# Key sums of six batches turned by a transposing DMA instead of TensorE, in a fused linear-attention and MoE kernel

## Chip, cores and metric

One Trainium2 chip, one core. The metric is the device time of one launch in microseconds (us). Most executions of a kernel agree within 0.3%. Engines are called PE (TensorE), DVE (VectorE), ACT (ScalarE), Pool (GpSimd) and SP (the queue that issues most DMAs).

## The reference

```python
def phi(x):                       # 8 batches, 8 heads, 576 tokens, 64 wide, 128 features
    proj = einsum('bhsd,md->bhsm', x, omega)
    h = proj - sum(x * x, -1, keepdims=True) / 2
    h = h - max(h, -1, keepdims=True)
    return exp(h) / sqrt(m)
q_p, k_p = phi(q * scale), phi(k * scale)
kv = einsum('bhsm,bhsd->bhmd', k_p, v)      # the key sums
z = sum(k_p, axis=2)
attn = einsum('bhsm,bhmd->bhsd', q_p, kv) / (einsum('bhsm,bhm->bhs', q_p, z)[..., None] + 1e-6)
x = attn as (4608 tokens, 512)
logits = xn @ en.T / tau          # rows of x and expert_emb (8 experts) normalized
idx = argmax(logits); gate = softmax(logits)[idx]
out[t] = gate[t] * relu(x[t] @ w1[idx[t]]) @ w2[idx[t]]       # 512 -> 1024 -> 512
```

## The kernel before

**Two stages.** In the first, the attention runs over 36 tiles of 128 tokens, four superblocks of nine tiles, each of two batches; its rows of x are scattered to memory by expert. In the second, the experts run over 38 steps of 128 sorted rows. The change touches the first stage alone.

**One pass of the loop.** Pass i works on the keys of tile i and on the queries of tile i - 7. From pass 7 to pass 35 PE projects both query halves (line 374), turns the query features of the tile before (`qtr`, line 462), projects both key halves, adds one half of the heads of tile i - 1 to the key sums (`kvmm`, line 406), multiplies turned query features with finished key sums (`num`, line 482) and adds the other half of the heads. DVE takes the row maxima (line 378) and divides (`num_out`, lines 495 to 501); ACT does the exponentials (line 388, sixteen a pass) and a copy (line 467). Pool does the routing in small pieces (`routed`) and scatters one tile's rows a pass (line 570). SP issues the loads of keys, values and queries some two passes ahead, as buffers come free.

**The key sums.** A batch (a "half", b = 0 or 1, of superblock sb) is complete behind pass i = 5, 9, 14, 18, 23, 27, 32 and 36. `kv_out` (line 420) then copies its sums from PSUM into the tile `kvs`: 128 features by 8 heads by 64 sums, the denominator, and 8 columns that hold the product of the sums with the normalized expert rows, so that `num` gives numerators, denominator and expert logits together. For these 8 columns the sums have to be turned, from features by channels to channels by features, two heads at a time: `kv_dense` (Pool, line 424) packs 64 of each 73 columns into the tile `xgp[2]`; two passes later, `kv_turn` (PE, line 433, four transposes into a PSUM bank), `kv_turned` (DVE, line 437, one copy back to `xgp[2]`), `kv_logits` (PE, line 444, sixteen small products) and `kv_logits_out` (DVE, line 450, into `kvs`). Pass i + 2 is called the turning pass here: passes 11, 16, 20, 25, 29 and 34 for the six halves of the change. They begin at 39.93, 67.11, 88.12, 115.16, 136.16 and 165.53 us.

**Order.** PE, Pool and SP run their instructions as written; DVE and ACT too inside the loop. Work that isn't done at once is put into lists, `early`, `spare`, `mid` and `ends`, keyed by pass and slot, and `go` runs a list: `early` at the start of a pass, `ends` at its end. In a turning pass PE has `kv_turn` between the first `kvmm` and `num`, and `kv_logits` right behind `num`. The scatter of a pass (line 570) is written in `ends`, so it stands on Pool's queue ahead of whatever `early` of the next pass brings. `xgp[0]` is free from pass 7 to pass 35.

Of the kernel before, what the change touches and what calls it, by code (L numbers as in the profile page):

```python
# [15 lines left out]
U16 = mybir.dt.uint16  # L16
# [6 lines left out]
P = 128  # L23
B, H, S, D, M = 8, 8, 576, 64, 128
E, F = 8, 1024
N = B * S
DM = H * D
# [12 lines left out]
NPRE = 2  # L40
# [24 lines left out]
def attention_moe(ctx: ExitStack, tc: tile.TileContext, qT, kT, v1, omT, emb, tau, w1q, w2q, xs, out):  # L65
    nc = tc.nc
# [56 lines left out]
    first = const.tile([P, 1], F32, name="first")  # L123
    firsti = const.tile([P, NPRE + 2], I32, name="firsti")
    xgp = [const.tile([P, PAY], F32, name=f"xgp{t}") for t in range(NPRE + 1)]
# [197 lines left out]
    with ExitStack() as c1:  # L323
# [5 lines left out]
        kva, kvs, st = {}, {}, {}  # L329
# [5 lines left out]
        def load(i):  # L335

            if i >= NTILE:
                return
            if i == LAG - 1:
                st["k", i] = xgp[0][:, 0:DM].rearrange("p (c m) -> p c m", c=4)  # L340
            else:
                st["k", i] = p1.tile([P, 4, P], F32, name=f"kt{i}", tag="qt" if i in (2, 3) else "kt", bufs=2)
            nc.sync.dma_start(st["k", i], kT[i])
# [17 lines left out]
        def loadq(i):  # L361
            if 0 <= i < NTILE:
                st["q", i] = p1.tile([P, 4, P], F32, name=f"qt{i}", tag="kt" if i in QLOADS[NTILE][1:] + QLOADS[NTILE + 1] else "qt", bufs=2)
                nc.sync.dma_start(st["q", i], qT[i])
# [3 lines left out]
        def proj(*which):  # L368
            for w, i, a, k in which:
                st["pj" + w, i, a] = (pb[k] if isinstance(k, int) else k).rearrange("p (c m) -> p c m", c=4)  # L370
            for c in range(4):
                for w, i, a, _ in which:
                    r = slice(a * D, (a + 1) * D)
                    nc.tensor.matmul(st["pj" + w, i, a][:, c, :], st[w, i][r, c, :], om[r, :], start=True, stop=True)  # L374
# [39 lines left out]
        def kv_out(sb, b):  # L414
            for a in range(2):
                to, acc = kvs[sb, b][:, 4 * a : 4 * a + 4, 0 : D + 1], kva[sb, b, a]
                if (sb, b) == (0, 0):
                    nc.vector.tensor_copy(to, acc)
                else:
                    nc.scalar.activation(to, acc, AF.Copy)  # L420
# [14 lines left out]
        def kv_turned(sb, b):  # L435
            kvt = xgp[NPRE][:, 0:DM].rearrange("p (c m) -> p c m", c=4)
            nc.vector.tensor_copy(kvt.rearrange("p c m -> p (c m)"), st["kvb"])
            st["kvt", sb, b] = kvt

        def kv_logits(sb, b):  # L440
            st["kve", sb, b] = pe = nu[1][:, 424 : 424 + 8 * E].rearrange("p (c e) -> p c e", c=4)
            for c in range(4):
                for o in range(0, P, 64):
                    nc.tensor.matmul(
                        pe[o : o + 64, c], st["kvt", sb, b][:, c, o : o + 64], enbd[:, c].rearrange("p a e -> p (a e)"),
                        start=True, stop=True,
                    )
# [148 lines left out]
        def first_weights(n):  # L596

            if n == 0:
                st["fe"] = nc.values_load(firsti[0:1, NPRE + 1 :], engines=[ET.SP], min_val=0, max_val=E - 1, skip_runtime_bounds_check_because=WHY)
            q, wn = n // 2, ("w1", "w2")[n % 2]  # L600
            st["rf", n] = raw = rawp.tile([P, F], F32, name=f"rf{n}", tag=f"raw_{wn}")
            nc.sync.dma_start(raw, W[wn][0].rearrange("(e q) p f -> e q p f", q=NQ)[ds(st["fe"], 1), q].rearrange("o p f -> (o p) f"))
# [123 lines left out]
        early, spare, mid, ends, behind = {}, {}, {}, {}, []  # L726
# [9 lines left out]
        def go(d, *key):  # L736
            for f, *a in d.pop(key, ()):
                f(*a)
# [6 lines left out]
        loop.enter_context(tc.manual_schedule(engines={ET.DVE, ET.Activation}))  # L745
        for i in range(NTILE + LAG + 2):
            iq = i - LAG
            for n in QLOADS.get(i, () if i >= NTILE else (iq + 2,) if i >= LAG else (i - 4,)):
                loadq(n)
            ahead = i + (4 if i < 2 else 2)  # L750
            if i < 2 or i > 4:
                load(ahead)
            if i in LOADS:
                first_weights(LOADS[i])
            if i == 1 or i >= 4:
# [10 lines left out]
            ks, qs = i < NTILE, 0 <= iq < NTILE  # L766
            st["both"] = ks
            sb, u = divmod(i - 1, TPS)
# [10 lines left out]
            if ks and qs:  # L779
                if i > LAG:  # L780
                    proj(q1 + (3,), q0 + (1,))
                if turns:
                    qtr(iq - 1, *nu)
                maxima(*q1)
                if turns:
                    qcopy(iq - 1, 1)
                    qcopy(iq - 1, 0, True)
                maxima(*q0)
                go(spare, i, 4)
                feats(*q1)  # L790
                feats(*q0)
                proj(k1 + (2,), k0 + (0,))
                maxima(*k1)
                maxima(*k0)
                kv(1)
                if u == 4:
                    kv(0)
                    kv_out(sb, 0)
                go(spare, i, 3)
                slot(4)  # L800
                if sums:
                    num(iq - 1)
                go(spare, i, 0)
                go(spare, i, 1)
                slot(2)
                if u == 4:
                    kv(0, 1, b=1)
                else:
                    kv(0)
                if sums:  # L810
                    num_out(iq - 1)
                feats(*k1)
                feats(*k0)
                slot(0)
                slot(1)
            elif ks:
                for j in KPROJ.get(i, ()):
                    proj(*keys(j))
                if i == LAG - 1:
                    proj(("q", 0, 1, 3), ("q", 0, 0, 1))  # L820
                go(spare, i, 0)
                maxima(*k0)
                maxima(*k1)
                slot(0)
                if i == LAG - 1:
                    kv_out(0, 0)
                    kv_dense(0, 0)
                    for a in range(2):
                        kvmm(i - 2, a, 1)
                    kv(0, 1)  # L830
                    kv_turn(0, 0)
                    emb2()
                else:
                    kv(0, 1)
                slot(1)
                feats(*k0)
                go(spare, i, 1)
                feats(*k1)
                slot(2)
            else:  # L840
                mine, other = ((3, 1), (0, 2))[:: 1 if i % 2 == NTILE % 2 else -1]
                if qs:
                    proj(q1 + (mine[0],), q0 + (mine[1],))
                kv(1)
                go(spare, i, 2)
                slot(3)
                if turns:
                    qtr(iq - 1, *(pb[k] for k in other))
                kv(0)
                if sums:  # L850
                    num(done)
                go(spare, i, 0)
                if i == NTILE + 1:
                    flush()
                if qs:
                    maxima(*q1)
                    maxima(*q0)
                if i > NTILE and turns:
                    qcopy(iq - 1, 0, True)
                if qs:  # L860
                    feats(*q1)
                if i == NTILE:
                    kv_out(sb, 1)
                    qcopy(iq - 1, 0, True)
                if qs:
                    feats(*q0)
                if turns:
                    qcopy(iq - 1, 1)
                if sums:
                    num_out(done)  # L870
                flush()
                filled(1)
                slot(0)
                slot(1)
                filled(FILLS[i] - 1)
                go(spare, i, 1)
                slot(2)
            if sums and done % G == G - 1:
# [16 lines left out]
                for n, (d, *key) in enumerate(plan):  # L895
                    todo = at(d, *key) if key[0] < NTILE + LAG + 2 else behind
                    todo.insert(0 if n == 0 else len(todo), (next, steps, None))
            go(ends, i)
            if 0 <= i - 1 < NTILE and u in (4, 8):
                b = u // 4 - 1  # L900
                if b and ks:
                    kv_out(sb, b)
                k = int(not ks)
                if i + 2 == LAG:
                    todo = (kv_turned, spare, i + 2, 4), (kv_logits, spare, i + 2, 3), (kv_logits_out, mid, i + 2, 4)
                else:
                    kv_dense(sb, b)
                    todo = (kv_turn, spare, i + 2, 3 - k), (kv_turned, mid, i + 2, 4 - k)
                    todo += (kv_logits, spare, i + 2 + k, 0), (kv_logits_out, mid, i + 2 + k, 0)
                for f, *key in todo:  # L910
                    at(*key).append((f, sb, b))
# [184 lines left out]
    with tc.manual_schedule(engines={ET.PE, ET.Activation, ET.DVE, ET.Pool, ET.SP}):  # L1096
# [82 lines left out]
        for t in range(NPRE, NSTAT):  # L1179
# [10 lines left out]
            early = late and (t < SHIFT or t == ends)  # L1190
# [105 lines left out]
    with tc.If(tot > NSTAT):  # L1296
        with tc.For_i(NSTAT, tot, 1) as i:
            get = lambda k, eng, mx: nc.values_load(tabi[k : k + 1, ds(i, 1)], engines=[eng], min_val=0, max_val=mx, skip_runtime_bounds_check_because=WHY)
            xgl = x_of("x", get(0, ET.SP, DUM))
            src = get(2, ET.SP, E * NQ - 1)  # L1300
# [65 lines left out]
```

## Time and profile before

| | |
|---|---|
| median of 3 runs | 640.89 us (640.69 to 641.74) |
| profiled execution | 637.09 us, span from first to last instruction 635.4 us |
| PE, DVE, ACT, Pool busy | 98%, 77%, 68%, 66% of the span |
| first stage | to about 200 us |

The profile shows one execution. Its busy shares are means over both stages, so a term of the first stage has to be read from the stretches there.

### The profile page before, as it was taken

How to read it: one execution, taken by the hardware profiler on the slowest of the kernel's cores; microseconds unless marked ns; L12 is line 12 of the kernel's file. 1: busy time of each engine (PE TensorE's matmuls, PEld its weight loads, DVE VectorE, ACT ScalarE, POOL GpSimd, SP SyncE). 2: the span in 40 equal slices, each digit the busy share in tenths (PEclk: the TensorE clock that was granted, in tenths of full speed). 3: DMA queues.
4: the chain of work that ended last, by engine and by line, in shares of the span. 5: the costliest groups of instructions: out<-in, count | busy, mean ns of one | idle time of the engine just before them, and what ended most of it. 6: DMA issues, size and time to landing. Idle time of an engine off the chain costs nothing.

```text
span 635.4 us, 19064 instructions
## 1 busy us (share of the span) xinstructions
PE 622.5 (98%) x6293; PEld 532.9 (84%) x6294; DVE 490.5 (77%) x908; ACT 433.2 (68%) x1139; POOL 421.9 (66%) x603
## 2 busy tenths in 40 slices
PE   8999999999999899999999999999999999999996
PEld 8999999988878788888888888888888888888885
DVE  5788888888879834797778776888877787878754
ACT  6999899898998327665666675666575657576630
POOL 3013344455777734579787888989797979787962
PEclk9999999999999999999999999999999999999999
DMA  7654766767682377798978687787878686868631
GB/s 257 210 149 158 231 202 200 222 200 256 233 289 80 142 267 233 233 230 224 214 222 230 206 227 223 204 244 191 243 191 239 198 243 188 239 203 223 198 117 46
DMA packets 142239, 131.93 MB, mean 208 GB/s; under 512 B 106742, under 2 KB 106870, under 8 KB 142144
## 3 DMA queue, kind: packets, MB, share of 16 engines
q1 hardware_dynamic: 135520, 109.70, 60.1%
q0 software_dynamic: 6480, 20.91, 8.6%
q8 instruction: 57, 0.93, 0.6%
q14 instruction: 38, 0.31, 0.1%
q10 hardware_dynamic: 144, 0.07, 0.0%
HBM read 83.78 MB, written 21.97 MB: 166 GB/s over the span
## 4 chain that ended last, share of the span: by engine, by line
PE 69%; ACT 3%; DVE 2%; issue 0%; POOL 0%; ACTq 0%; DVEq 0%
PE pb L285 31%; PE po L285 31%; PE fs_o L285 2%; PE pb L374 1%; ACT ftq L388 1%; PE nuu L482 1%; PE pb L267 1%; PE fs_a L285 1%; PE kva L406 1%; DVE nmq L378 0%; PE pb L462 0%; ACT qp L467 0%; DVE xr L501 0%; DVE rt_p L299 0%; DVE qp L469 0%
## 5 line engine op out<-in xcount | busy, mean ns | idle before, releaser
L240 POOL TENSOR_TENSOR w2l<-raww,w2h 128x256 f32 x128 | 144.4, 1128 | 7.6
L240 POOL TENSOR_TENSOR w1l<-raww,w1h 128x256 f32 (+1 forms) x130 | 112.9, 869 | 14.0 <-DMA xgp<-xs 4.8
L285 PE MATMUL po<-w2h,hh 128*128 (+1 forms) x288 | 112.2, 390 | 0.0
L285 PE MATMUL po<-w2h,hl 128*128 (+1 forms) x288 | 112.1, 389 | 0.0
L285 PE MATMUL po<-w2l,hh 128*128 (+1 forms) x288 | 112.0, 389 | 0.0
L285 PE MATMUL pb<-w1h,xh 128*128 (+1 forms) x280 | 109.4, 391 | 0.0
L285 PE MATMUL pb<-w1h,xl 128*128 (+1 forms) x280 | 109.0, 389 | 0.0
L285 PE MATMUL pb<-w1l,xh 128*128 (+1 forms) x280 | 109.0, 389 | 0.0
L1086 DVE COPY pl<-pb 128x512 uint16<-128x512 uint16 x68 | 46.8, 690 | 61.5 <-ACT pl L1082 61.4
L1082 ACT ACTIVATE pl<-pb 128x512 uint16<-128x512 uint16 x68 | 39.5, 586 | 75.4 <-PE pb L285 71.3
L388 ACT ACTIVATE ftq<-pb,nmq 128x128 f32<-128x128 f32 x288 | 79.7, 414 | 2.2 <-DVE nmq L378 2.2
L315 POOL DMA_INDIRECT y<-xgp,tail x36 | 44.9, 1247 | 53.3 <-DVE w1h L234 29.5
L388 ACT ACTIVATE ftk<-pb,nmk 128x128 f32<-128x128 f32 x272 | 75.9, 460 | 4.8 <-DVE nmk L378 4.8
L1104 DVE COPY wd<-t 128x1024 uint16<-128x1024 uint16 x68 | 65.0, 959 | 1.3 <-DMA t<-pl 1.2
L1120 ACT ACTIVATE hh<-wd 128x1024 fp32r<-128x1024 f32 x34 | 36.1, 1063 | 42.4 <-DVE wd L1104 37.4
L285 PEld LDWEIGHTS po<-w2h,hl 128*128 128x128 f32 x288 | 54.1, 188 | 11.3
L285 PEld LDWEIGHTS po<-w2h,hh 128*128 128x128 f32 x288 | 54.1, 188 | 11.2
L285 PEld LDWEIGHTS po<-w2l,hh 128*128 128x128 f32 x288 | 54.0, 188 | 11.0
L285 PEld LDWEIGHTS pb<-w1h,xl 128*128 128x128 f32 x280 | 52.5, 188 | 10.9
L285 PEld LDWEIGHTS pb<-w1h,xh 128*128 128x128 f32 x280 | 52.6, 188 | 10.9
L285 PEld LDWEIGHTS pb<-w1l,xh 128*128 128x128 f32 x280 | 52.6, 188 | 10.7
L1124 DVE SCALAR_TENSOR_TENSOR hl<-wd,hh 128x1024 fp32r<-128x1024 f32 x34 | 54.2, 1594 | 4.0 <-ACT hh L1120 3.4
(341 smaller groups left out, 1242.9 us busy)
## 6 DMA issues: line engine op xcount, KB each, us to landing
raww<-w1q SPq DMA_DIRECT2D x38, 512.0 KB, 4.0
raww<-w2q SPq DMA_DIRECT2D x38, 512.0 KB, 4.8
qt<-qT SPq DMA_DIRECT2D x36, 256.0 KB, 4.1
kt<-kT SPq DMA_DIRECT2D x35, 256.0 KB, 3.6
xg<-xs SPq DMA_DIRECT2D x23, 260.5 KB, 2.8
xgp<-xs SPq DMA_DIRECT2D x15, 260.5 KB, 4.8
rf<-w1q SPq DMA_DIRECT2D x4, 512.0 KB
rf<-w2q SPq DMA_DIRECT2D x4, 512.0 KB
```

Of the source, the lines that this page charges most:

```text
L240: ils.append(eng.tensor_tensor(at(l, d)[:, c], raw[:, c], at(h, d)[:, c].bitcast(F32), op=ALU.subtract))
L267: nc.tensor.transpose(bank[:, c * P : (c + 1) * P], src[:, o + c * P : o + (c + 1) * P], ident)
L285: done.append(nc.tensor.matmul(dst, x[:, c * P : (c + 1) * P], ws.rearrange("p o f -> p (o f)"), start=(begin and i == 0 and k == 0), stop ...
L315: w = nc.gpsimd.indirect_dma_start(out=out, out_offset=bass.IndirectOffsetOnAxis(ap=(xg[:, DM:] if tail is None else tail)[:, E : E + 1].b ...
L374: nc.tensor.matmul(st["pj" + w, i, a][:, c, :], st[w, i][r, c, :], om[r, :], start=True, stop=True)
L388: nc.scalar.activation(ft[:, h, :], pj[:, h, :], AF.Exp, bias=nm[:, h : h + 1])
L406: nc.tensor.matmul(acc[c : c + 64, h, :], ft[:, h, c : c + 64], vt[:, 2 * h + a, :], start=begin and h == 0, stop=u == 4 + 4 * b and h == 3,)
L1082: nc.scalar.activation(planes[1][:, o : o + 512], halved(src)[:, :, 1], AF.Copy)
L1086: nc.vector.tensor_copy(planes[0][:, o : o + 512], halved(src)[:, :, 0])
L1104: nc.vector.tensor_copy(to, src)
L1120: nc.scalar.activation(hh, wd[:, 0:F], AF.Relu)
L1124: nc.vector.scalar_tensor_tensor(hl, wd[:, 0:F], 0.0, hh.bitcast(F32), op0=ALU.max, op1=ALU.subtract)
```

## The change

For the six halves that finish behind passes 9 to 32, PE's four transposes and DVE's copy are dropped. In their place, Pool splits the packed sums into two planes of 16-bit words (low and high halves of each 32-bit number) in `xgp[2]` (`kv_planes`, two copies of 128x512); SP issues one transposing DMA of 128x1024 words from there into `xgp[0]` (`kv_spun`, in pass i + 1); Pool joins the two turned planes into 32-bit numbers in `xgp[2]` (`kv_joined`, two copies of 128x512, first of its work of pass i + 2). `kv_logits` and what follows are as before. For b = 0 the planes are filled directly behind `kv_out`, in the middle of pass i, and the DMA is issued ahead of the loads of pass i + 1; for b = 1 at the end of pass i, and ahead of the value load of pass i + 1.

```diff
+        def kv_planes(sb, b):
+            pl = xgp[NPRE][:, 0:DM].bitcast(U16).rearrange("p (k c a d) -> p k a c d", k=2, a=2, d=D)
+            src = kvs[sb, b].bitcast(U16).rearrange("p (a c) (w two) -> p a c w two", a=2, two=2)
+            for k in range(2):
+                nc.gpsimd.tensor_copy(pl[:, k], src[:, :, :, 0:D, k])
+
+        def kv_spun(sb, b):
+            st["t16", sb, b] = t16 = xgp[0][:, 0:DM].bitcast(U16).rearrange("p (f m) -> p f m", m=P)
+            nc.sync.dma_start(t16, xgp[NPRE][:, 0:DM].bitcast(U16), transpose=True)
+
+        def kv_joined(sb, b):
+            st["kvt", sb, b] = xgp[NPRE][:, 0:DM].rearrange("p (c m) -> p c m", c=4)
+            to = xgp[NPRE][:, 0:DM].bitcast(U16).rearrange("p (c m two) -> p c m two", c=4, two=2)
+            for k in range(2):
+                nc.gpsimd.tensor_copy(to[:, :, :, k], st["t16", sb, b][:, 4 * k : 4 * k + 4])
...
+            go(early, i, "first")
             for n in QLOADS.get(i, () if i >= NTILE else (iq + 2,) if i >= LAG else (i - 4,)):
                 loadq(n)
             ahead = i + (4 if i < 2 else 2)
             if i < 2 or i > 4:
                 load(ahead)
+            go(early, i, "spin")
...
                 if u == 4:
                     kv(0)
                     kv_out(sb, 0)
+                    kv_planes(sb, 0)
...
                 if i + 2 == LAG:
                     todo = (kv_turned, spare, i + 2, 4), (kv_logits, spare, i + 2, 3), (kv_logits_out, mid, i + 2, 4)
+                elif ks:
+                    if b:
+                        kv_planes(sb, b)
+                    todo = (kv_spun, early, i + 1, "spin" if b else "first"), (kv_joined, early, i + 2)
+                    todo += (kv_logits, spare, i + 2, 0), (kv_logits_out, mid, i + 2, 0)
                 else:
                     kv_dense(sb, b)
                     todo = (kv_turn, spare, i + 2, 3 - k), (kv_turned, mid, i + 2, 4 - k)
```

## Rows read from the trace of the kernel before

**Rows 1.** The page: busy time by engine; one costly group; one group of loads.

```profile
PE 622.5 (98%) x6293; PEld 532.9 (84%) x6294; DVE 490.5 (77%) x908; ACT 433.2 (68%) x1139; POOL 421.9 (66%) x603
...
L1104 DVE COPY wd<-t 128x1024 uint16<-128x1024 uint16 x68 | 65.0, 959 | 1.3 <-DMA t<-pl 1.2
...
kt<-kT SPq DMA_DIRECT2D x35, 256.0 KB, 3.6
```

**Rows 2.** Waits of ACT, 36 to 176 us: total us, times, longest us.

```profile
ACT qp L467 <- PE nuu L462: 8.3, 12, 1.7
ACT qp L467 <- DVE nmq L378: 3.7, 3, 1.5
```

**Rows 3.** Timeline of turning pass 16: start us, length us, then the instruction.

```profile
69.71 0.69 PE L406 MATMUL kva<-vt15v,ftk 128*64 128x65 f32 x16
...
70.20 1.04 POOL L570 DMA_INDIRECT xs<-xr,posi  x1 [0.54 <-issue]
...
71.13 1.25 PE L482 MATMUL nuu<-kvs,qp 128*64 128x73 f32 x32
...
72.21 0.59 PE L444 MATMUL nuu<-enbd,xgp 128*64 128x16 f32 x16
...
72.92 0.17 DVE L495 TENSOR_SCALAR rr<-nuu 128x8 f32<-128x8 f32 x1 [0.92 <-PE nuu L444]
...
75.12 0.60 ACT L467 ACTIVATE qp<-nuu 128x512 f32<-128x512 f32 x1 [1.54 <-DVE nmq L378]
```

**Rows 4.** Lines 424 and 437: count, ns min/median/max, first and last start.

```profile
L424 POOL COPY xgp<-kvs x8: 612/620/642, 19.8 to 183.6; 128x512 f32<-128x512 f32 x8
...
L437 DVE COPY xgp<-pb x6: 692/692/693, 44.4 to 169.7; 128x512 f32<-128x512 f32 x6
```

**Rows 5.** Line 1092, 240 to 300 us: the second stage's transposing DMAs, issue and landing.

```profile
L1092 SPq DMA_TRANSPOSE t<-pl x11: 1237/1307/2394, 250.3 to 299.1; - x11
...
DMA to landing us min/median/max: 2.8/2.8/2.8
```

**Rows 6.** Pool groups by shape, whole span: busy us, mean ns, idle before.

```profile
L232 POOL TENSOR_TENSOR w2l<-raww,w2h 128x1024 fp32r<-128x1024 f32 x4 | 9.5, 2396 | 9.6 <-ACT w2h L230 9.6
...
masks.py:199 POOL TENSOR_SCALAR_AFFINE_SELECT ident<-ident 128x128 f32<-128x128 f32 x1 | 0.3, 282 | 0.0
L97 POOL TENSOR_SCALAR_AFFINE_SELECT tri<-one 128x128 bf16<-128x128 bf16 x1 | 0.3, 282 | 0.0
```

**Rows 7.** Timeline of Pool near the turning passes 11, 20, 29 and 34.

```profile
37.30 0.61 POOL L424 COPY xgp<-kvs 128x512 f32<-128x512 f32 x1 [16.62 <-ACT kvs L420]
...
87.59 0.62 POOL L424 COPY xgp<-kvs 128x512 f32<-128x512 f32 x1
...
90.15 1.00 POOL L570 DMA_INDIRECT xs<-xr,posi  x1 [0.49 <-DVE nmq L378]
...
136.84 0.20 POOL L586 TENSOR_TENSOR cnt<-isf,iote 128x8 f32<-128x8 f32 x1 [0.47 <-DVE rr L495]
...
141.15 1.06 POOL L570 DMA_INDIRECT xs<-xr,posi  x1 [0.50 <-DVE nmk L378]
...
163.52 2.78 POOL L617 TENSOR_TENSOR w2l<-rf,w2h 128x256 fp32r<-128x256 f32 x4
...
168.62 1.04 POOL L570 DMA_INDIRECT xs<-xr,posi  x1 [0.54 <-issue]
```

**Rows 8.** Timeline of PE in the turning passes 11, 20, 29 and 34.

```profile
43.62 0.66 PE L433 MATMUL pb<-ident,xgp 128*128 128x128 f32 x4
...
93.33 0.59 PE L444 MATMUL nuu<-enbd,xgp 128*64 128x16 f32 x16
...
142.08 0.59 PE L444 MATMUL nuu<-enbd,xgp 128*64 128x16 f32 x16
...
170.63 0.59 PE L444 MATMUL nuu<-enbd,xgp 128*64 128x16 f32 x16
```

**Rows 9.** Timeline of SP in pass 15.

```profile
64.80 0.33 SPq L343 DMA_DIRECT2D kt<-kT  x1
```

## The prediction

> **What bounds the kernel now.** I read the page first: PE is busy 98% of the span [rows 1], but that is a mean over two stages, so it doesn't yet say what a PE instruction of the first stage is worth. Next came the waits of ACT in the first stage: ACT stands idle 8.3 + 3.7 = 12.0 us between 36 and 176 us, all of it at its query copy [rows 2]. Last the timelines, pass by pass. There the reader is to see two kinds of passes. Between the turning passes ACT runs its exponentials back to back and sets the pace. In a turning pass PE does, its work being longer by the transposes and the small products. ACT, which ran ahead, waits for it at the start of the next pass, 1.54 us behind pass 16 [rows 3]. So time is won or lost in a turning pass by one thing: when `kv_logits` (line 444) ends. DVE's division (line 495) waits for it 0.92 us [rows 3], PE's next `qtr` waits for that division, ACT for `qtr`. If line 444 starts later by x, everything behind is later by x. If it starts earlier by x, all is earlier by x, up to what ACT waits there.
>
> **What is removed.** Four transposes per half. In pass 11 they are listed with 0.66 us [rows 8], and a listed length reaches a little into the next group (line 482's to 72.38, where line 444 starts at 72.21 [rows 3]): 0.6 us of PE. In pass 16 the first `kvmm` ends at 69.71 + 0.69 = 70.40 and `num` starts at 71.13 [rows 3]: with a wait ahead of the transposes 0.73 us, some 0.8 with the overlap. I take 0.6 for passes 11 and 20 and 0.8 for the four others: line 444 could start 4.4 us earlier in sum. DVE's copy, 0.69 us [rows 4], goes too; DVE waited 0.92 us after it, so this alone is worth nothing. Pool's packing copy, 0.62 us, goes [rows 4].
>
> **What is added on Pool.** Four copies of 128x512 16-bit words per half. No row shows a 16-bit copy on Pool. Nearest is the copy that goes: the same count, 32-bit, 0.62 us [rows 4]; and a Pool pass over 128x128 costs 282 ns in 16 bits as in 32 [rows 6], so Pool seems to pay by the element. I take 0.62. Lower bound: DVE's pass over twice as many 16-bit words, 0.96 us, halved: 0.48, rounded down to 0.45 [rows 1]. Upper bound: Pool's two-operand pass over 1024 elements, 2.40 us, halved is 1.20 [rows 6]; one operand lies between that and 0.62, so 0.95.
>
> The row gives 0.62 us for a Pool copy of 512 elements [rows 4]. [...]
>
> **What is added on SP.** One transposing DMA per half: 1.31 us of issue and 2.8 us from issue to landing for 128x1024 words [rows 5]; up to 3.4 where loads are in the ring (an estimate, 2.8 and a fifth). For b = 0 it waits for the planes, filled in the middle of pass i, and stands ahead of the three loads of pass i + 1; for b = 1 it holds only the value load and those of the next pass. Loads have room: the key tile issued at 64.80 [rows 9] lands 3.6 us later [rows 1], at 68.4, and is first read in pass 17, later than 72.92 [rows 3], over 4.5 us of cover against 1.3 to 2 us of delay. So nothing for SP; without that cover it would be up to 2 us a half.
>
> **When the join is done, half by half.** `kv_joined` is written first in pass i + 2, but Pool runs in order, and the scatter of pass i + 1 (line 570) stands ahead of it. I take the join as two copies, 1.24 us, and 0.07 us until PE starts: 1.31 behind whatever holds it.
>
> - Pass 16: the scatter ends at 70.20 + 1.04 = 71.24 [rows 3]; planes and DMA, of passes 14 and 15, are long done. Line 444 can start at 72.55; it started at 72.21. **+0.34**. PE would have been ready at about 71.4.
> - Pass 25 repeats pass 16 row for row: **+0.34**.
> - Pass 34: the scatter ends at 169.66 [rows 7]; Pool is full ahead of it (the weight pieces of line 617 from 163.52 are followed without a gap), so the extra copy pushes it by about 0.3. 169.96 + 1.31 = 171.27 against 170.63 [rows 8]: **+0.6**.
> - Pass 29: in pass 28 Pool has the choice of the first expert, from 136.84 on [rows 7], and the scatter ends at 142.21. The extra copy, 0.62, less the 0.47 of idle ahead of line 586, pushes that by 0.15. 142.36 + 1.31 = 143.67 against 142.08 [rows 8]: **+1.6**.
> - Pass 20: planes start at 87.59 [rows 7], where the packing copy did, and end at 88.83; the DMA is issued near 88.9 and lands at 91.7 to 92.3. The scatter, pushed by 0.62, ends at 91.77. With 92.0: 92.0 + 1.31 = 93.31 against 93.33 [rows 8]: **0.0** (-0.25 to +0.3).
> - Pass 11: planes from 37.30 [rows 7] to 38.54, landing 41.4 to 42, joined by 43.3. `num` would start near 43.62 [rows 8] and takes 72.21 - 71.13 = 1.08 [rows 3], to 44.7, so no wait: **-0.6**.
>
> Sum: 0.34 + 0.34 + 0.6 + 1.6 + 0.0 - 0.6 = +2.3 us. PE's saved time is spent waiting for Pool. The profiled execution goes from 637.09 to 639.4; the median stands 3.8 above it, and I carry that over: 640.89 + 2.3 = **643.2**.
>
> At the copy's lower bound (0.45, so join and start 0.97) passes 16, 25 and 34 come to 0.0, pass 20 to -0.6, pass 29 to +1.1, pass 11 to -0.6: -0.1, 640.8. At the upper (0.95; 1.97) passes 16 and 25 give +1.0 each, pass 20 +1.3, 29 +3.0 (pushed by 0.8), 34 +2.1, 11 -0.6: +7.8, 648.7.
>
> **Rivals.** *The join is in time* (the other side): Pool reaches it before `num` ends in all six, and line 444 starts when PE is ready: -4.4 us, 636.5. For it: Pool is busy 66% of the span [rows 1] and less here, and both planes and DMA are ready a pass early for b = 0. Against: order, not load. It decides at the point where the join ends by about 71.4 in pass 16, which is 0.16 us behind the scatter; only if Pool starts the join before the scatter's listed end can two copies fit.
>
> *Nothing measurable*: copies near the lower bound, or one or two joins that slip ahead of the scatter's end: the sum lies within 1.3 us of zero, 640.8. For it: three of six halves lie within 0.34 of break-even. Against: pass 29, where 1.1 us stay lost at any price of a copy.
>
> *Dearer copies*: writing every second 16-bit word, or waiting between two copies into the same tile, costs Pool more than a 32-bit copy: up to 648.7. For it: no row of such a copy. Against: the two 282 ns rows [rows 6]. [...]
>
> *Loads late*: the loads behind the transposing DMA reach PE late and a projection waits; 1 us a half gives 640.89 + 2.3 + 6 = 649. Against: the cover of 4.5 us.
>
> **How the numbers follow.** 0.2% is 1.28 us, about what a measurement of this kernel tells from no change. The joins late at about the row's price, with a copy between 0.55 and 0.72 (642.2 to 644.6): 0.46. Dearer copies: 0.12. Loads late: 0.03. Nothing measurable: 0.23. In time, wholly or mostly: 0.16. Thus faster 0.16, same 0.23, slower 0.46 + 0.12 + 0.03 = 0.61. The range 638.5 to 646.5 leaves out the larger gains (0.10) and the dearest copies and late loads (0.08); the likeliest case alone is 642.2 to 644.6.
>
> **What the profile after would show.** PE idle ahead of line 444 in passes 16, 25, 29 and 34, released by Pool's join, longest in pass 29 (over 2 us) and none in pass 11; each join starting where the scatter ends; its two copies near 0.62 us; ACT's wait at line 467 behind those passes longer than 1.54 us; no wait of PE for a load. Wrong is the prediction if the join runs ahead of the scatter, if a 16-bit copy costs under 0.4 us or over 0.8, or if line 495 doesn't follow line 444 any more.

## The result and the profile after

The changed kernel takes 644.14 us (median of 6 runs, 643.69 to 645.27), the kernel before 640.79 beside it (639.41 to 641.74): ratio 1.0053, 95% interval 1.0042 to 1.0063, so 3.35 us slower, where 643.2 (+2.3) was forecast. Chips differ here by as much as the change does: the kernel before took 641.65 us on the chip of the first experiments, 641.76 on that of the second and 637.32 on that of the third, so each experiment has its ratio to the kernel before on its own chip. The changed kernel itself was run only beside the runs above: where an experiment is held against it below, two ratios or two profiles are compared, not two times on one chip. The profile of before that the prediction used (637.09) is like the third chip's runs, the profile after (644.21, span 642.5) is like the others'.

The page of the changed kernel, its busy times. Against [rows 1] GpSimd's is 10.9 us higher, DVE's 1.5 lower and PE's no lower, though 24 transposes are gone: a mean over the span says little here.

```profile
PE 623.8 (97%) x6269; PEld 532.9 (83%) x6270; DVE 489.0 (76%) x902; ACT 432.0 (67%) x1139; POOL 432.8 (67%) x621
```

Waits of the changed kernel, 36 to 182 us, of PE and then of ACT (total us, times, longest us). The answer to [rows 2]: ACT still waits at its query copy (now line 483), 18.8 us in place of 12.0 (16.4 for the kernel before in the first experiment below), and PE has a wait that the kernel before doesn't have, at the logits (now line 460), in five of six halves:

```profile
PE nuu L460 <- POOL xgp L454: 5.9, 5, 2.4
...
ACT qp L483 <- PE nuu L478: 13.4, 11, 3.9
ACT qp L483 <- DVE nmq L378: 5.4, 3, 2.1
```

Timelines of the changed kernel in passes 11, 16, 20, 29 and 34 (start us, length us, instruction), the answers to [rows 3, 7, 8]. Line 586 is the scatter, 454 the join, 460 the logits, 511 DVE's division, 374 the start of a pass:

```profile
44.99 0.59 PE L460 MATMUL nuu<-enbd,xgp 128*64 128x16 f32 x16
...
67.05 1.16 PE L374 MATMUL pb<-om,qt 64*128 64x128 f32 x16
...
70.14 1.04 POOL L586 DMA_INDIRECT xs<-xr,posi  x1 [0.54 <-issue]
71.20 1.43 POOL L454 COPY xgp<-xgp 128x512 uint16<-128x512 uint16 x2
...
72.68 0.65 PE L460 MATMUL nuu<-enbd,xgp 128*64 128x16 f32 x16 [0.84 <-POOL xgp L454]
...
73.45 0.17 DVE L511 TENSOR_SCALAR rr<-nuu 128x8 f32<-128x8 f32 x1 [2.12 <-PE nuu L460]
...
73.77 1.16 PE L374 MATMUL pb<-om,qt 64*128 64x128 f32 x16
...
91.42 1.00 POOL L586 DMA_INDIRECT xs<-xr,posi  x1 [0.49 <-DVE nmq L378]
93.40 1.42 POOL L454 COPY xgp<-xgp 128x512 uint16<-128x512 uint16 x2 [0.98 <-DMA xgp<-xgp]
...
94.87 0.65 PE L460 MATMUL nuu<-enbd,xgp 128*64 128x16 f32 x16 [0.91 <-POOL xgp L454]
...
144.64 1.06 POOL L586 DMA_INDIRECT xs<-xr,posi  x1 [0.51 <-DVE nmk L378]
145.71 1.43 POOL L454 COPY xgp<-xgp 128x512 uint16<-128x512 uint16 x2
...
147.19 0.65 PE L460 MATMUL nuu<-enbd,xgp 128*64 128x16 f32 x16 [2.40 <-POOL xgp L454]
...
176.96 0.65 PE L460 MATMUL nuu<-enbd,xgp 128*64 128x16 f32 x16 [0.96 <-POOL xgp L454]
```

In pass 16 the scatter ends at 71.18, the join starts at 71.20 and ends at 72.63, PE starts at 72.68: scatter, join, logits, with no gap. The division then starts at 73.45, and DVE waits 2.12 us for it in place of 0.92 [rows 3]. Pass 29 has the longest wait, 2.40 us, pass 11 none. In pass 20 it isn't the scatter (ended at 92.42) but the transposing DMA that the join waits for.

The lines of the change over the whole span (count, ns min/median/max, first and last start), the answer to [rows 4, 5]: the copies that fill the planes cost what the packing copy cost (0.61 us), those that join them a quarter more (0.76):

```profile
L444 POOL COPY xgp<-kvs x12: 603/608/621, 37.8 to 166.7; 128x512 uint16<-128x512 uint16 x12
...
L454 POOL COPY xgp<-xgp x12: 743/758/777, 42.9 to 176.2; 128x512 uint16<-128x512 uint16 x12
...
L448 SPq DMA_TRANSPOSE xgp<-xgp x6: 1233/1387/1989, 39.0 to 167.3; - x6
```

### The profile page after: what moved, and what is told of

It is laid out like the page before. It is cut to its first block, busy times and chain, and to the rows that moved or that the text cites. A ratio compares the mean times of both kernels' runs of the same rounds, so it can differ in the third digit from the quotient of the medians.

```text
span 642.5 us, 19045 instructions
## 1 busy us (share of the span) xinstructions
PE 623.8 (97%) x6269; PEld 532.9 (83%) x6270; DVE 489.0 (76%) x902; ACT 432.0 (67%) x1139; POOL 432.8 (67%) x621
## 4 chain that ended last, share of the span: by engine, by line
PE 84%; ACT 5%; POOL 4%; DVE 3%; DMA 2%; issue 2%; SPq 0%; POOLq 0%; ACTq 0%; DVEq 0%
PE pb L285 31%; PE po L285 30%; PE pb L374 7%; PE kva L406 4%; PE nuu L498 4%; PE nuu L478 2%; ACT ftq L388 2%; PE fs_o L285 2%; POOL xgp L454 1%; POOL xs L586 1%; ACT ftk L388 1%; PE pb L267 1%; DMA kt<-kT 1%; PE fs_a L285 1%; DMA vt<-v 1%
## 5 line engine op out<-in xcount | busy, mean ns | idle before, releaser
L1128 DVE COPY wd<-t 128x1024 uint16<-128x1024 uint16 x68 | 67.3, 993 | 1.1 <-DMA t<-pl 1.1
L285 PEld LDWEIGHTS pb<-w1l,xh 128*128 128x128 f32 x280 | 52.5, 188 | 10.9
```

The lines of the kernel that those rows point to most:

```text
L285: done.append(nc.tensor.matmul(dst, x[:, c * P : (c + 1) * P], ws.rearrange("p o f -> p (o f)"), start=(begin and i == 0 and k == 0), stop ...
L1128: nc.vector.tensor_copy(to, src)
```

## The experiments

A pass is measured below from one start of its query projection (line 374) on PE to the next one, in the profiles.

**The kernel before again**, on the chip of the first three experiments, with a profile: 639.92 us, span 638.3.

> The kernel before, unchanged, profiled once more. The changed kernel's profile shows waits that the profile of before did not: in every third pass (15, 18, 21, 24, 27, 30) the query copies of ACT and DVE start some 0.7 us after the listed end of the transposes that they read, some 3 us in sum with what follows. Theory A: these waits belong to executions, not to the change; then a profile of before with a time near 640.8 us shows them too. Theory B: they come from the change; then this profile has none, whatever its time.

Theory A holds: the waits are there without the change. In pass 18 the query copy starts 0.86 us after the listed end of the transposes that it reads; the lines stand in the last section. So this is the profile to hold against the one after, with single executions on both sides. Its pass 16, from one projection to the next:

```profile
66.61 1.16 PE L374 MATMUL pb<-om,qt 64*128 64x128 f32 x16
...
71.94 0.64 PE L444 MATMUL nuu<-enbd,xgp 128*64 128x16 f32 x16
...
73.03 1.16 PE L374 MATMUL pb<-om,qt 64*128 64x128 f32 x16
```

The lengths, in us:

| Pass | before again | changed | difference | forecast |
|---|---|---|---|---|
| 11 | 6.37 | 5.62 | -0.75 | -0.6 |
| 16 | 6.42 | 6.72 | +0.30 | +0.34 |
| 20 | 6.37 | 6.75 | +0.38 | 0.0 |
| 25 | 6.40 | 6.72 | +0.32 | +0.34 |
| 29 | 6.62 | 8.20 | +1.58 | +1.6 |
| 34 | 6.43 | 6.72 | +0.29 | +0.6 |
| sum | | | +2.12 | +2.28 |
| 15, 24, 33 | 15.07 | 15.70 | +0.63 | 0 |

From the start of pass 11 to that of pass 36 it is 139.27 us before and 142.47 after, +3.20: the turning passes, the three passes ahead of the halves b = 0, and 0.45 in passes 27, 28 and others.

**The join ahead of the scatter.** The join is written at the end of pass i + 1, ahead of the scatter and behind that pass's routing piece.

```diff
-todo = (kv_spun, early, i + 1, "spin" if b else "first"), (kv_joined, early, i + 2)
+todo = (kv_spun, early, i + 1, "spin" if b else "first"), (kv_joined, joins, i + 1)
...
+if (i,) in joins:
+    last = at(ends, i)
+    if sums and done % G == G - 1:
+        f, *a = last.pop(0)
+        f(*a)
+    go(joins, i)
 go(ends, i)
```

> The changed kernel with the join written one place earlier on Pool's queue: ahead of the scatter of pass i + 1, behind that pass's routing. Theory 1 (Pool's order is the cause): the products with the expert rows start about 0.9 us earlier in passes 16, 25 and 34 and 1.55 us earlier in pass 29; pass 20, where the DMA's landing holds the join, and pass 11 stay. Sum 4.3 us: about 639.8 us, ratio to before 0.998 to 0.999. Theory 2 (the transposing DMA in the load queue costs the time, by loads or waits elsewhere): little is gained, 643 to 644.5 us.

Measured: 641.8 us, ratio 1.0003 (0.999 to 1.0016). The loss is gone, but no gain has come. The turning passes are 2.6 us shorter than before (pass 16 5.88, pass 34 5.77, pass 29 6.80), the passes behind them longer: 21 by 0.49, 30 and 31 by 0.72 together, 15, 24 and 33 by 0.2 each. Its timeline of pass 20 and 21:

```profile
92.85 0.65 PE L460 MATMUL nuu<-enbd,xgp 128*64 128x16 f32 x16 [0.20 <-POOL xgp L454]
...
92.92 1.01 POOL L586 DMA_INDIRECT xs<-xr,posi  x1
...
94.33 0.17 DVE L511 TENSOR_SCALAR rr<-nuu 128x8 f32<-128x8 f32 x1 [1.55 <-PE kva L406]
...
95.77 0.71 PE L478 MATMUL nuu<-ident,ftq 64*128 64x64 f32 x16 [0.68 <-DVE kvs L466]
```

The logits are listed to 93.50, but DVE's division behind them starts at 94.33, 0.40 us after the end of the scatter, which the join has pushed onto this place (the profile names the second `kvmm`, listed to 94.01, as the last to release it; how a scatter and such a start go together is in the last section). So `qtr` waits 0.68 us for DVE: what the logits gained is lost in the next step. The experiment wasn't run on the third chip, where the trace of pass 18 has no such start (last section).

**Both ahead.** As the join ahead, with the copy of the sums and the planes of the halves b = 1 ahead of the scatter too.

```diff
+if ks and i - 1 > 0 and u == 8:
+    kv_out(sb, 1)
+    kv_planes(sb, 1)
 if (i,) in joins:
...
-if b and ks:
-    kv_out(sb, b)
```

> As the join ahead of the scatter, and for the halves b = 1 (turning passes 11, 20, 29) the copy of the sums and the planes are written ahead of the scatter of the pass too, so that the transposing DMA of pass 20 lands some 1 us earlier. If the loss is Pool's order alone, pass 20 falls from 6.01 us to about 5.6 and pass 29 by 0.3, and the time stands 0.7 us below the join ahead of the scatter: ratio to the kernel before 0.999. If what the turning passes give is taken back in the passes behind them, because the scatters come later (rival), the ratio stays at 1.000 and passes 21 and 30 grow by what 20 and 29 lose.

Measured: 642.22 us, ratio 1.0017 (1.0001 to 1.0034). The gain expected for Pool's order alone hasn't come, and the ratio is nearer to the rival's. Against the join ahead, pass 20 falls by 0.22 to 5.79 and pass 29 by 0.20 to 6.60; 19 grows by 0.40 to 5.61 and 21 by 0.09 to 5.97, while 30 stays at 6.09: what was won is given back, but mostly not where the rival had it. Pass 25 is 6.84 in place of 5.88; PE waits 0.28 us for the join there, and three joins of the run wait for the DMA, 3.1 us in sum.

**Pass 11 alone, and pass 29 back on PE.** One keeps the change for the half of pass 11 alone, the other for all but that of pass 29.

```diff
-elif ks:
+elif i == 9:
...
-elif ks:
+elif ks and i != 27:
```

> The change for one half alone, that of turning pass 11, where Pool has nothing ahead of the join; the five others are turned by PE as before. Theory 1: that pass gets 0.6 to 0.8 us shorter and nothing else moves: 640.1 us, ratio about 0.999. Theory 2: the DMA costs more than PE's transposes give, 641 us or more.

> The changed kernel with the half of turning pass 29 back on PE, the five others by DMA. In that pass PE waited 2.4 us for the join, behind the choice of the first expert on Pool. Theory 1: the pass goes from 8.2 back to about 6.95 us: 642.9 us, ratio 1.003 to 1.0035. Theory 2: a sixth of the loss goes, 643.6 us.

Measured: pass 11 alone 641.14 us, ratio 0.9993 (0.9978 to 1.0008); its pass 11 is 5.65, 0.72 shorter than before, the other turning passes 6.34 to 6.72 as before, and passes 15, 24 and 33 are 5.02, 4.98 and 5.04. The time can't tell the two theories apart, since the interval holds both no change and 0.999; the trace shows the first. All but pass 29: 642.78 us, ratio 1.0015 (1.0004 to 1.0026), against 1.0053 with it, so more came back than either theory had: pass 29 is 6.47 in place of 8.20, pass 30 0.4 longer, and passes 15, 24 and 33 stay at 5.24, 5.15 and 5.25. The two passes give 1.3 us; the ratios, from two chips, differ by 2.4, and the rest isn't traced.

**The join made twice over.**

```diff
-for k in range(2):
+for k in (0, 1, 0, 1):
     nc.gpsimd.tensor_copy(to[:, :, :, k], st["t16", sb, b][:, 4 * k : 4 * k + 4])
```

> The changed kernel with the join's two copies made twice over (the second pair writes the same words). Theory (the join behind the scatter sets the logits): 1.43 us more in each of the turning passes 16, 20, 25, 29 and 34 and 0.7 to 1.4 in pass 11, where the join ended 0.65 us ahead of the logits: 7.8 to 8.6 us more than the changed kernel's 644.1, about 652, ratio 1.018. Rival (the logits wait for something else, and the wait for the join is one that others would take up): under 3 us more, ratio below 1.010.

Measured: 657.38 us, ratio 1.0231 (1.0194 to 1.0268). The loss follows the dose: the turning passes 11 to 29 are 0.92, 1.33, 1.62, 1.66 and 1.38 longer than in the changed kernel, and pass 34 is 2.30 longer. By the ratios it is 11.4 us in all, more than the 8.6 expected. The six runs lie between 652.25 and 661.61, and the profile is of the slowest; in it passes 17, 21, 26, 30 and 35, behind the turning ones, are 5.8 us longer in sum. In the five stretches of 20 us that hold them PE's granted clock is 0.83 to 0.91, in the four others from 36 to 210 us it is 1.00. Timeline of PE and, in the second fence, stretches from 76 to 82 us (stretch, length, busy us and count of PE, PEld, DVE, ACT, POOL; granted clock, DMA share, GB/s):

```profile
77.98 0.65 PE L460 MATMUL nuu<-enbd,xgp 128*64 128x16 f32 x16 [2.14 <-POOL xgp L454]
...
79.06 1.98 PE L374 MATMUL pb<-om,qt 64*128 64x128 f32 x16
```

```profile
76.00:77.50 1.50, 0.00 (x0) 0.00 (x0) 0.00 (x0) 1.50 (x6) 1.50 (x3) 1.00 0.63 247
...
80.50:82.00 1.50, 1.50 (x24) 1.50 (x24) 0.74 (x2) 0.05 (x1) 1.01 (x2) 0.50 0.35 128
```

After the 2.14 us wait the granted clock stands at 0.50 (1.00 before it), the projection takes 1.98 us in place of 1.16, and pass 17 is 6.23 in place of 4.82.

**The join in Pool's gap.** Both ahead, with the halves b = 0 joined a pass earlier, where GpSimd stood idle from 64.06 to 68.07 in the profile of the changed kernel.

```diff
-(kv_joined, joins, i + 1)
+(kv_joined, *((joins, i + 1) if b else (spare, i + 1, 1)))
```

> The halves b = 0 (turning passes 16, 25, 34) are joined a pass earlier, in the gap that Pool has from 64.1 to 68.1 us in pass 15, so that neither the join waits for a scatter nor a scatter for the join; the halves b = 1 as with both ahead. Theory: passes 16, 25 and 34 are 0.5 to 0.6 us shorter than the kernel before's and the passes behind them no longer, 15, 24 and 33 stay 0.2 longer; pass 11 -0.75; passes 20 and 29 with those behind them even. Sum about -1.8: 639.0, ratio 0.997. Rival (the transposing DMA lands too late for the gap, or its time in the ring costs): the join waits for the DMA, the next routing piece and the scatter wait behind it, ratio 1.000 or above.

Measured: 642.77 us, ratio 1.0012 (0.9998 to 1.0027); the rival holds. Its timeline of pass 15, SP and GpSimd:

```profile
62.81 1.24 SPq L448 DMA_TRANSPOSE xgp<-xgp  x1
...
70.13 1.44 POOL L454 COPY xgp<-xgp 128x512 uint16<-128x512 uint16 x2 [6.78 <-DMA xgp<-xgp]
```

From issue to join it is 7.3 us, 6.1 and 5.1 in the other two, not the 2.8 of [rows 5]: the join holds up the routing pieces and the scatter behind it (73.72 in place of 69.70 in the kernel before), and pass 18 is 6.21. Passes 25 and 34, at 5.63 and 5.49, are as short as was hoped; passes 27, 29 and 35, at 6.07, 7.39 and 5.83, are not.

**The join on DVE**, ahead of the key maxima of the turning pass.

```diff
-    nc.gpsimd.tensor_copy(to[:, :, :, k], st["t16", sb, b][:, 4 * k : 4 * k + 4])
+    nc.vector.tensor_copy(to[:, :, :, k], st["t16", sb, b][:, 4 * k : 4 * k + 4])
...
-(kv_joined, early, i + 2)
+(kv_joined, spare, i + 2, 4)
```

> The join is made by VectorE (two copies of 128x512 16-bit words, ahead of the key maxima of the turning pass); GpSimd keeps the planes. VectorE's 0.96 us over 1024 such words gives 1.0 to 1.2 us for the two. Theory (the loss is the wait of GpSimd's join behind the scatter): the logits follow num without a wait, the turning passes are 0.6 us shorter than the kernel before's in each half, 3.6 us in sum, less 0.6 us in passes 15, 24 and 33, where the planes stay: 637.8, ratio 0.995. Rival (the loss comes with the transposing DMA, the planes or VectorE's own load): no gain over the kernel before, ratio 1.000 or above, with the key maxima and the key features behind them as late as the join is long.

Measured: 639.43 us, ratio 0.9964 (0.9947 to 0.9981): faster than the kernel before, where the changed one is slower. The same again on the third chip:

> The join on VectorE once more, for the comparison with the planes at the end: ratio 0.995 to 0.998 if the gain is one of the kernel and not of one chip.

Measured: 635.26 us, ratio 0.9965 (0.9951 to 0.9979). On the second chip the turning passes take 5.64, 5.67, 5.60, 5.65, 5.82 and 5.55, 4.7 us less in sum than in the kernel before on the first chip; passes 30 and 33, 0.5 and 1.0 longer, take part of it back. The copies' line and pass 16 of that profile:

```profile
L454 DVE COPY xgp<-xgp x12: 442/452/585, 43.3 to 169.7; 128x512 uint16<-128x512 uint16 x12
```

```profile
70.04 0.79 DVE L454 COPY xgp<-xgp 128x512 uint16<-128x512 uint16 x2
...
71.64 0.63 PE L460 MATMUL nuu<-enbd,xgp 128*64 128x16 f32 x16
...
72.39 0.17 DVE L511 TENSOR_SCALAR rr<-nuu 128x8 f32<-128x8 f32 x1 [0.40 <-PE nuu L460]
```

DVE needs 0.79 us for both copies, GpSimd 1.43; the logits have no wait, since `num` is listed to 71.85. With the join off GpSimd's queue, its order and its dearer copies are both gone, and so is the loss; that the order does most of it rests on the join ahead, at the same price of a copy.

**The planes at the end of the pass**, where the packing copy stood, for the halves b = 0: once with the join on GpSimd as changed, once with the join on DVE.

```diff
 kv_out(sb, 0)
-kv_planes(sb, 0)
...
-if b:
-    kv_planes(sb, b)
+kv_planes(sb, b)
-(kv_spun, early, i + 1, "spin" if b else "first")
+(kv_spun, early, i + 1, "spin")
```

> The changed kernel with the planes of the halves b = 0 filled at the end of the pass, where the packing copy stood, behind the scatter; the transposing DMA then stands behind the loads of the next pass's start. Theory (the planes ahead of the scatter are what makes passes 15, 24 and 33 longer by 0.2 us each): these fall back to 5.03, 4.98 and 5.06, the turning passes stay as in the changed kernel (6.72, 6.75, 8.20): 0.6 us less than the changed kernel, about 643.5, ratio 1.004. Rival (those passes differ for another reason): they stay at 5.2 to 5.3. If the transposing DMA now lands behind the scatter of the turning pass, passes 16, 25 and 34 grow.

> The join on VectorE as before, and the planes of the halves b = 0 at the end of the pass. Theory: passes 15 and 24 lose 0.2 us each and pass 33, where VectorE's operation of 128x24 took 1.61 us in place of 0.17 while GpSimd filled the planes, up to 1.0: 1.0 to 1.4 us less than the join on VectorE alone, ratio to the kernel before 0.994 to 0.995. Rival: the later DMA makes VectorE wait for it in passes 16, 25 and 34 and takes the gain back: ratio 0.996 or above.

Measured on the third chip: 643.77 us, ratio 1.0101 (1.008 to 1.0123), and 636.25 us, ratio 0.9979 (0.9964 to 0.9993). In both the theory misses. Passes 15, 24 and 33 of the first are 4.97, 4.97 and 4.98; but 15 and 24 are 4.98 on this chip with the planes in the middle too, so that on it the planes' place costs these two nothing. The changed kernel wasn't run there, so what the move alone does to the time isn't settled. In pass 34 the logits wait 1.95 us, behind a scatter that the planes and four weight pieces push, and the pass is 8.11, with PE's clock at 0.50 behind the wait. In the second kernel DVE waits for the later DMA, as the rival has it, but of the rival's three passes in pass 16 alone: issued at 64.81, and the join starts at 71.35. That pass is 6.67, where it is 5.15 with the join on DVE alone on this chip; passes 25 and 34 have no such wait (5.17 and 5.49, as with the join on DVE alone). Its timeline of pass 16:

```profile
71.35 0.79 DVE L454 COPY xgp<-xgp 128x512 uint16<-128x512 uint16 x2 [1.57 <-DMA xgp<-xgp]
...
72.28 0.65 PE L460 MATMUL nuu<-enbd,xgp 128*64 128x16 f32 x16 [1.27 <-DVE xgp L454]
```

**The transposing DMA twice**, for the halves b = 0, the second into a tile that nobody reads.

```diff
 nc.sync.dma_start(t16, xgp[NPRE][:, 0:DM].bitcast(U16), transpose=True)
+again = xgp[1][:, 0:DM].bitcast(U16).rearrange("p (f m) -> p f m", m=P)
+if b == 0:
+    nc.sync.dma_start(again, xgp[NPRE][:, 0:DM].bitcast(U16), transpose=True)
```

> The changed kernel with a second transposing DMA of the same planes behind the first, into a tile that nobody reads, for the halves b = 0 (passes 15, 24 and 33). Theory (the ring has room, the loads have cover, the join waits for the scatter): at most 0.3 us more in all, ratio to the kernel before 1.005 to 1.006 as the changed kernel. Rival (the transposing DMA delays the loads behind it, and this is part of the loss): 1 to 2 us more for each of the three, a projection waits for a load in passes 15 to 17, 24 to 26 and 33 to 35, ratio 1.009 to 1.015.

Measured on the third chip: 642.64 us, ratio 1.0091 (1.0065 to 1.0117). The number lies in the rival's range, the trace doesn't bear it out: PE waits for no load from 36 to 182 us, and the kernel with single DMAs and the planes at the end has 1.0101 on that chip. Part of the time has another cause: in pass 29, whose half has a single DMA, PE waits 2.45 us for the join and the projection behind it takes 2.08 us; passes 29 and 30 are 9.37 and 5.92, against 8.77 and 5.16 with the planes at the end, where the wait is 2.46 and the projection takes 1.16. What the second DMA costs is seen once, in pass 25, where the join (line 457 here) waits 0.51 us for it and the pass is 7.21 in place of 6.72:

```profile
120.44 1.42 POOL L457 COPY xgp<-xgp 128x512 uint16<-128x512 uint16 x2 [0.51 <-DMA xgp<-xgp]
...
145.54 0.82 PE L463 MATMUL nuu<-enbd,xgp 128*64 128x16 f32 x16 [2.45 <-POOL xgp L457]
...
147.24 2.08 PE L374 MATMUL pb<-om,qt 64*128 64x128 f32 x16
```

## Why the prediction was right, and where its terms were off

*The mechanism held.* The join starts where the scatter ends, the logits where the join ends, and the division, `qtr` and the query copy follow. Four experiments show it from different sides: doubled copies lengthen the turning passes by 0.9 to 2.3 us each; the join ahead of the scatter shortens them; the half of pass 29 back on PE takes 1.7 us off that pass; with the join taken off GpSimd, and DMA and planes kept, the kernel is 0.35% faster than before.

*The sum was right in part by luck: two errors cancel.* The terms were worked out on a profile of 637.09 us, whose pass 16 takes 6.13; on the chip of the first experiments it takes 6.42 before the change, and 6.72 in the profile after. The join copy, put at 0.62 (bounds 0.45 and 0.95), costs 0.76, and the join 1.43 in place of 1.24 (the 0.07 until PE starts came to 0.05): by its own base pass 16 should have come to 0.34 + 0.19 = +0.53. The third chip shows about that (6.73 with the planes at the end, against 6.13 in the profile of before, +0.60), and +1.82 in pass 29 (8.77 against 6.95), where 1.6 + 0.19 comes to 1.79. Against the longer pass before the change on the first chip, the forecast for pass 16, +0.34, came out at +0.30. In pass 34 the push of 0.3 on the scatter didn't come: it starts 3.12 us into the pass, 3.09 in the kernel before, and the pass is 0.29 longer, not 0.6. On the third chip both variants that keep the join on GpSimd lose 0.9 to 1.0%; what the changed kernel would lose there wasn't measured.

*Dearer copies.* The rival was right in sign and place for the join alone: the copy that writes every second word costs 0.76, the one that reads every second word 0.61.

*The DMA's landing was the weak term.* Put at 2.8 to 3.4 us, it took some 4.0 in pass 20 (issued at 89.39, join at 93.40) and, with the join in Pool's gap, 5.1 to 7.3 us from issue to join, behind four loads issued in the 2.5 to 3.5 us before it (that these loads make it longer is the author's estimate, no run leaves them out). So pass 20 came to +0.38 and not 0.0. In the halves b = 0 the scatter ended later still and hid it (pass 16: DMA issued at 63.38, scatter ended at 71.18).

*Loads late* fell: no projection waited for a load, in the changed kernel and with the DMA doubled.

*The join in time* fell as forecast, but for a second reason as well. The prediction said that a join ahead of the scatter's end would be worth 4.4 us. Put ahead of it, the turning passes do shorten, by 2.6, but DVE's division then starts only behind the scatter, and the passes behind lose most of it again.

*What was left out.* Some 0.6 us in passes 15, 24 and 33. They take 5.02, 4.98 and 5.04 with the change in pass 11 alone, and 5.24, 5.15 and 5.25 with all but pass 29's half, so it goes with the halves b = 0: in pass 15 the planes push the scatter from 0.79 to 1.06 us behind the pass's start, and the query copies start 0.20 later against `qtr`. With the DMA doubled on the third chip the planes stand at the same place, ACT's query copy starts 0.04 us behind the listed end of `qtr`, and the pass stays at 4.98: the push seems to cost only where such starts lie behind a scatter. Pass 33 is another case: DVE's line 546 takes 0.95 us beside the planes' copies, in place of 0.47, and its query copy starts 0.26 later. The remaining 0.5 us lie in passes whose length differs from run to run (pass 27: 5.25 us in the kernel before again, 5.38 in the profile of before, 5.57 with pass 11 alone).

## What to carry to other kernels

A step that needs an engine's answer at a fixed time shouldn't be queued behind an instruction there that nobody waits for, and swapping the two may only move the wait, as it did here on the two chips where it was tried. Look for an engine that idles at that very place: DVE waited 0.92 us [rows 3] for the step that the join was holding up. And take the landing of a DMA from a stretch like the one where it will run: it was 2.8 us in the second stage [rows 5], and 4.0 to 7.3 from issue to join in the first.

## What the runs showed of the hardware

*Starts behind a scatter, on some chips.* In the profile after and on the first two chips a DVE or ACT instruction that waits for PE while GpSimd runs an indirect scatter often starts some 0.4 us behind the scatter's end, long after PE's listed end. From 36 to 182 us, in the kernel before on the first chip, 13 starts that waited for PE lie 0.25 to 0.55 us behind the end of a scatter and 2 fall inside one; in the profile after it is 12 and 1, in the profile of before 2 and 7. With the join in Pool's gap, on the second chip, the query copies of passes 15, 17, 18 and 24 start 0.32 to 0.38 us behind one. Timelines around pass 18, of the kernel before on the first chip and then of the join on DVE on the third:

```profile
78.92 0.71 PE L462 MATMUL nuu<-ident,ftq 64*128 64x64 f32 x16
...
79.14 0.98 POOL L570 DMA_INDIRECT xs<-xr,posi  x1 [0.94 <-DVE sel L530]
...
80.49 0.60 ACT L467 ACTIVATE qp<-nuu 128x512 f32<-128x512 f32 x1 [0.86 <-PE nuu L462]
```

```profile
78.05 0.71 PE L478 MATMUL nuu<-ident,ftq 64*128 64x64 f32 x16
...
78.28 0.98 POOL L586 DMA_INDIRECT xs<-xr,posi  x1 [0.94 <-DVE sel L546]
...
78.81 0.60 ACT L483 ACTIVATE qp<-nuu 128x512 f32<-128x512 f32 x1
```

The same three instructions stand in the same order and distance; on the first chip the query copy starts 0.86 us after the listed end of `qtr` and 0.37 after that of the scatter, on the third 0.05 after `qtr` (0.04 in the profile of before, with the same kernel as on the first chip). Passes 19 and 28 differ as well, 4.68 us each in the profile of before and 5.14 and 5.01 on the first chip. Why the chips differ wasn't found, and that the scatter is the cause is read from these coincidences: no run leaves it out.

*A long DVE instruction beside GpSimd's.* In the join on DVE, pass 33 is 6.04 us in place of 5.06. Its timeline:

```profile
160.41 1.61 DVE L546 SCALAR_TENSOR_TENSOR sel<-raw,iotm 128x24 bf16<-128x24 f32 x1
...
160.80 1.16 POOL L444 COPY xgp<-kvs 128x512 uint16<-128x512 uint16 x2
```

The median of line 546 is 0.17 us; here it takes 1.61 and ends at 162.02, 0.06 behind the planes' copies, and PE's `num` then waits 0.85 us for DVE. GpSimd ran weight pieces (line 633, from 159.45 to 160.86) and the two copies one behind the other, and the DVE instruction, which starts beside a weight piece, ends only behind the last copy. In the changed kernel's pass 33 the same instruction ran from 165.82 to 166.77, 0.05 behind the end of the first of the two copies (166.12 to 166.72) and ahead of that of the second (167.29). In the kernel before on the first chip it (line 530 there) took 0.47 us, from 162.11 to 162.58, 0.05 behind the weight pieces (to 162.53), and in the profile of before 0.18, beside weight pieces that ran from 158.03 to 160.80. So its end lies 0.05 to 0.06 us behind that of a GpSimd instruction in three of these four profiles, and not always behind the last of a row. That GpSimd holds it up is read from these coincidences; no run shows how.

*PE's clock.* The granted clock stood at 0.50 behind waits of 2.14 us in pass 16 with the join made twice (80.50 to 82.00 us) and of 1.95 us in pass 34 with the planes at the end (176.50 to 178.00); behind the 2.45 us in pass 29 with the DMA doubled the projection took 2.08 us in place of 1.16. The clock stayed at 1.00 behind the 2.40 us of pass 29 in the changed kernel (147.00 to 150.00), and behind the 2.46 us of that pass with the planes at the end the projection took 1.16 us: a wait's length alone doesn't tell.
